# The last four token tiles of a down projection: two plain tiles, then a pair in seven products

## The chip, the core and the metric

The kernel runs on one core of a Trainium2 chip, in one launch. Time is device time in microseconds (us) of one execution; the kernel before took 725.91 us, the median of three runs (725.77 to 726.37). The engines are TensorE (PE, matrix products; its weight loads are listed as PEld), VectorE (DVE), ScalarE (ACT), GpSimd (POOL) and SyncE (SP), which issues the DMAs. Matrix products are accumulated in the banks of PSUM; all else that the engines work on lies in SBUF.

## The reference

One layer of an FNet block and a gated feed-forward block, on x of 2048 tokens by 448:

```
a = x_n @ dft_hid_re.T ; b = x_n @ dft_hid_im.T        # x_n = layernorm(x)
h = x + dft_seq_re @ a - dft_seq_im @ b
g = layernorm(h) @ w_gate ; u = layernorm(h) @ w_up    # 448 -> 1792
out = h + (gelu(g) * u) @ w_down                       # 1792 -> 448
```

All values are f32. The part that this document is about is the last product, called "down", for the last 512 tokens.

## The kernel before

**Precision.** f32 operands are split into two f16 parts, a high part (the value rounded) and a low part (what is left), so that one product takes three f16 matmuls: high x high, high x low, low x high. `hi_part` (L102) makes the high part on ScalarE, `lo_part` (L105) the low part on VectorE.

**Stages.** First the sequence and hidden DFT, up to about 330 us; then, in a loop of 56 steps over t (L979), gate and up: four groups q of 512 tokens by 14 chunks f of the 1792 hidden values. The down projection runs inside the same loop, one step of it for each step t from 14 on.

**Down in seven products.** Tokens are taken in pairs of tiles of 128 and the 448 output columns in two halves (HD = 224); the 1792 hidden values, 14 chunks of 128, are taken as 7 pairs of chunks (NC = 7). So one pair of token tiles is a 2 x 2 block product with 2 x 2 blocks, and `STRASSEN` (L147) lists seven products that replace the eight. Their left operands are the quarters A11 and A22 themselves and five sums of quarters, their right operands likewise the weights' (`wd`, made once and kept in SBUF, seven forms of each chunk). For a step d, `dn_sums` makes the five sums of a chunk pair (L804: two instructions on GpSimd, one on VectorE), `dn_split` their high and low parts, `dn_mm` the 21 matmuls of 224 columns. Six pairs p = 0 to 5 (the first 1536 tokens) are done so, seven steps each. The seven results lie in four PSUM banks, and `Drain` (L607) adds them into the four quarters of the output rows `hr`: `copy` moves two banks to SBUF on ScalarE, `sums` adds the four products in them by eight instructions on GpSimd, `bank2` and `bank3` add the other three on VectorE from PSUM. The method `banks01`, which adds four of the terms of the first two banks on VectorE instead, is there and is not called. The drain of pair p is hung into later steps of the loop through the table `side` (L947 to L959); that of the sixth pair, p = 5, falls on the last step, t = 55, and on what stands behind the loop.

**The last four tiles.** The last group, q = 3, has no later steps of the loop to run down in. Its hidden values are split into f16 as they come (`last_hi`, `last_lo`, into `h_last`), and behind the loop four tiles of 128 tokens are multiplied plainly by `last_mm` (L867): 14 chunks x 3 terms x 2 column halves, 84 matmuls of 224 columns for a tile. A tile is called by (j, g): the tokens g * 256 + j * 128 and on; j picks the rows `hr[6 + j]`. The weights that the seven-product form does not hold in plain form (quarters 12 and 21) are kept in `w_last`. The tiles go one after the other, (0,0), (0,1), (1,0), (1,1), each into a PSUM bank of its own; the last one is done half by half, in two banks, so that the first half can be added and stored under the second. `last_out` (L886) adds a bank into `hr` on VectorE and issues the store on SyncE.

**Order.** The program is scheduled by hand: each engine runs its instructions in the order in which they stand in the code, and waits only for what an instruction needs. Tiles of SBUF come from pools with a fixed number of buffers for a tag; a new tile waits until the last users of the old one are done. The tags that matter here: `hh` (two buffers, the hidden values of a group, and `h_last`), `hq` (two buffers, the hidden values of one step of the last group), `dn_s` (two buffers, five sums).

The code behind the loop:

```
    prev.c_last()
    for k in (1, 2, 0, 3):
        do(N_GU, k)
    ...
    for i in range(4):
        j, g = divmod(i, 2)
        last_mm(j, g, banks[i : i + 1] if i < 3 else banks[3:5])
```

Of the kernel before, what the change touches and what calls it, by code (L numbers as in the profile page):

```python
# [8 lines left out]
F16 = mybir.dt.float16  # L9
F32 = mybir.dt.float32  # L10
AF = mybir.ActivationFunctionType
ALU = mybir.AluOpType

P = 128
S, D, DF = 2048, 448, 1792
NT = S // P
NF = DF // P
# [10 lines left out]
W_SC = 256.0  # L28
H_SC = 0.25
# [3 lines left out]
def kernel(  # L33
# [6 lines left out]
    w_down: bass.AP,  # L40
    out: bass.AP,
):

# [23 lines left out]
    nc = tc.nc  # L69
    V, A, G, PE = nc.vector, nc.scalar, nc.gpsimd, nc.tensor  # L70
# [7 lines left out]
    ps_tr = ctx.enter_context(tc.tile_pool(name="ps_tr", bufs=1, space=bass.MemoryType.PSUM))  # L78
# [23 lines left out]
    def hi_part(dst, src, scale=1.0):  # L102
        A.activation(dst, src, AF.Copy, scale=scale)  # L103

    def lo_part(dst, src, hi, scale=1.0):  # L105
        if isinstance(scale, float) and scale == 1.0:
            V.tensor_sub(dst, src, hi)  # L107
        else:
            V.scalar_tensor_tensor(dst, src, scale, hi, op0=ALU.mult, op1=ALU.subtract)  # L109
# [37 lines left out]
    STRASSEN = [(0, 5), (1, 4), (3, 0), (2, 1), (6, 6), (5, 3), (4, 2)]  # L147
    HD = D // 2
# [349 lines left out]
    def at(where, n, *what):  # L498
        where.setdefault(n, []).extend(what)
# [5 lines left out]
    for k, f in enumerate(reversed(range(NF))):  # L505
        n = 17 + 3 * k
# [4 lines left out]
    for b in range(NB):  # L511
        for j in range(2):
            n = (b + 1) * NT + 1 + 6 * j
# [41 lines left out]
    for n in range(N_STEPS):  # L555
        b, c = divmod(n, NT)
# [42 lines left out]
    fpool = ctx.enter_context(tc.tile_pool(name="fpool", bufs=1, side="right", reuse_waits="tile"))  # L599
    wd = {n: fpool.tile([P, 2, 7, HD], F16, name=f"wd{n}") for n in range(NF // 2)}  # L600
# [99 lines left out]
    TQ = 2 * P  # L700
# [25 lines left out]
    def ftile(tag, bufs, name, n=TQ):  # L726
        return (fpool if tag == "u1" else late).tile([P, n], F32, tag=tag, bufs=bufs, name=name)

    hh, hq = {}, {}
# [67 lines left out]
    NC = NF // 2  # L797
    dn_s, dn_w, acc_d, hr = {}, {}, {}, {}
# [5 lines left out]
    def dn_sums(d):  # L804
        t = dn_hid(d)
        s = dn_s[d] = late.tile([P, 5, P], F32, tag="dn_s", bufs=2, name=f"dn_s{d}")
        G.tensor_add(s[:, 0:2], t[:, 0:2], t[:, 2:4])
        G.tensor_sub(s[:, 2:4], t[:, 1:4:2], t[:, 0:4:2])  # L808
        V.tensor_add(s[:, 4], t[:, 0], t[:, 3])
# [7 lines left out]
    outr = out.rearrange("(k g j p) d -> k j p g d", k=2, g=2, j=4)  # L817
# [19 lines left out]
    def dn_drain(p):  # L837
        v = [ftile(f"v{k}", 1, f"v{k}_{p}", D) for k in range(2)]
        return Drain(hr[p], acc_d.pop(p), v, 1.0 / (H_SC * W_SC))

    def dn_store(p):
        nc.sync.dma_start(outr[p // 4, p % 4], hr[p])
# [3 lines left out]
    last = {}  # L846
# [20 lines left out]
    def last_mm(j, g, banks):  # L867

        tok = slice(g * TQ + j * P, g * TQ + (j + 1) * P)
        one = len(banks) == 1  # L870
        for cs in ((0, 1),) if one else ((0,), (1,)):
            for f in range(NF):
                k, n = divmod(f, NC)
                for m, (lh, lw) in enumerate(((0, 0), (0, 1), (1, 0))):
                    for c in cs:
                        w = wd[n][:, lw, k] if c == k else last["w"][:, lw, n, k]
                        PE.matmul(  # L877
                            banks[0][:, c * HD : (c + 1) * HD] if one else banks[c][:, 0:HD],
                            last["h"][:, lh, f, tok],
                            w,  # L880
                            start=f == 0 and m == 0 and c == cs[0],
                            stop=f == NF - 1 and m == 2,
                            skip_group_check=True,
                        )

    def last_out(j, g, ps, c, n):  # L886
        p = 6 + j
        h = hr[p][:, g, c * HD : (c + n) * HD]
        V.scalar_tensor_tensor(h, ps[:, 0 : n * HD], 1.0 / (H_SC * W_SC), h, op0=ALU.mult, op1=ALU.add)
        nc.sync.dma_start(outr[p // 4, p % 4][:, g, c * HD : (c + n) * HD], h)  # L890

    def dn_ahead(t):

        if t in (NF - 4, NF - 1):
            dn_sums(int(t == NF - 1))
        if NF <= t < 6 * NC + 12:
            dn_sums(t - 12)

    N_GU = 4 * NF
# [4 lines left out]
    def do(t, k):  # L904
        for what in side.pop((t, k), ()):
            what()
# [25 lines left out]
    for t in range(3 * NF, N_GU):  # L932
        f = t % NF
        if f < NF - 1:
            n, k = divmod(f, 2)
# [11 lines left out]
    for p in range(6):  # L947
        t0 = NF + NC * p + NC - 1

        def begin(p=p):  # L950
            drains[p] = dn_drain(p)
            drains[p].copy()
            drains[p].bank2()

        at(side, (t0, 2), begin)
        at(side, (t0 + 1, 0), lambda p=p: drains[p].bank3())
        for n in range(4):
            at(side, (t0 + 1 + n, 3), lambda p=p, n=n: drains[p].sums((2 * n, 2 * n + 1)))
        at(side, (t0 + 4, 3), lambda p=p: dn_store(p))  # L959
# [12 lines left out]
    late = ctx.enter_context(tc.tile_pool(name="late", bufs=1, reuse_waits="tile"))  # L972
    ps_gu = ctx.enter_context(tc.tile_pool(name="ps_gu", bufs=1, space=bass.MemoryType.PSUM, reuse_waits="tile"))
    ps_dn = ctx.enter_context(tc.tile_pool(name="ps_dn", bufs=1, space=bass.MemoryType.PSUM, reuse_waits="tile"))
# [4 lines left out]
    for t in range(N_GU):  # L979
        q, f = divmod(t, NF)  # L980
# [26 lines left out]
        if q == 0:  # L1007
            dn_ahead(t)
            cur.xy()
            if f == NF - 2:  # L1010
                dn_split(0)
            prev = cur
            cur = GateUp(t + 1)
            cur.open()
            prev.yz()
            if d == -1:
                prev.c12_plus()
            continue
# [3 lines left out]
        dn_mm(d, range(0, 8))  # L1022
        cur.xy()
        dn_ahead(t)
        dn_mm(d, range(8, 18))
        do(t, 1)
# [9 lines left out]
            cur = GateUp(t + 1)  # L1036
            cur.open()
    prev.c_last()
    for k in (1, 2, 0, 3):
        do(N_GU, k)  # L1040
    banks = [(ps_tr, "tr"), (ps_gu, "X"), (ps_gu, "Y"), (ps_gu, "Z"), (ps_dn, "a0")]
    banks = [pool.tile([P, 512], F32, tag=tag, name=f"last_{tag}") for pool, tag in banks]
    for i in range(4):
        j, g = divmod(i, 2)
        last_mm(j, g, banks[i : i + 1] if i < 3 else banks[3:5])
        if i < 3:
            last_out(j, g, banks[i], 0, 2)
        else:
            last_out(j, g, banks[3], 0, 1)
            last_out(j, g, banks[4], 1, 1)  # L1050
        for t in range(N_GU + 1, N_GU + 4) if i == 0 else ():
            do(t, 3)
    assert not side


# [57 lines left out]
```

## Time and profile before

| | us |
|---|---|
| median of three runs | 725.91 (725.77 to 726.37) |
| the profiled execution: its own time | 726.24 |
| its span, first to last instruction | 724.4 |
| TensorE busy in the span | 719.4 |
| VectorE, ScalarE, GpSimd busy | 499.7, 271.8, 233.7 |

The profile is of one execution. "Span" is the time from its first to its last instruction; its own time is 1.84 us longer. Lines of the profile name a line of the kernel (L877), which can be that of a helper (L107 is the VectorE instruction in `lo_part`, wherever it was called from), then engine and operation, the tile written and the tiles read, partitions x elements and types. In the timeline the first two numbers are the start and the duration in us, "x84" merges 84 instructions, and the bracket tells how long the engine had been idle and which instruction ended that. In the list of groups come the summed busy time and the mean of one in ns. In the table of stretches come, after the bounds and the length, the busy time and count of PE, PEld, DVE, ACT and POOL, then the clock granted to TensorE (1.00 is full), the share of the DMA engines' time, and GB/s. Matmuls overlap in the pipeline: each is recorded with 0.26 us here, and the pace is read from the starts.

### The profile page before, as it was taken

The page shows a single profiled execution, that of the slowest core. Times are in us where ns is not written, and L with a number is a line of the kernel's source. Part 1 is how long each engine was busy: PE and PEld are TensorE (multiplying, and loading weights), DVE is VectorE, ACT ScalarE, POOL GpSimd, SP SyncE. Part 2 cuts the span into 40 slices and gives each one's busy share as a digit, 9 for nine tenths or more (in the row PEclk, how much of TensorE's full clock was granted, in tenths as well). Part 3 has the DMA queues.
Part 4 walks back from the last instruction along what each step waited for, and adds up shares of the span by engine and source line. Part 5 has one row for each costly group of instructions (what it writes and reads, how often), then busy time and mean ns, then how long its engine had stood idle before and what let it go on. Part 6 is the DMA issues. An engine that isn't in the chain of part 4 may idle for free.

```text
span 724.4 us, 13422 instructions
## 1 busy us (share of the span) xinstructions
PE 719.4 (99%) x5330; PEld 500.6 (69%) x5330; DVE 499.7 (69%) x1026; ACT 271.8 (38%) x535; POOL 233.7 (32%) x274
## 2 busy tenths in 40 slices
PE   9999999999999999999999999999999999999998
PEld 5444444444444444444488889999999999999998
DVE  6888657486674856440567768787787877989730
ACT  4444704156132452130344444443444434444410
POOL 0000000000000001000148855577686766758430
PEclk9999999999999999999999999999999999999999
DMA  8676565578657876711643564747538596555411
GB/s 277 223 231 219 183 223 189 196 215 277 233 196 218 293 242 248 274 67 61 254 153 128 177 210 167 187 174 223 180 124 253 172 205 217 198 198 205 153 39 39
DMA packets 63518, 139.83 MB, mean 193 GB/s; under 512 B 30304, under 2 KB 39520, under 8 KB 63456
## 3 DMA queue, kind: packets, MB, share of 16 engines
q1 hardware_dynamic: 63456, 138.99, 57.8%
q8 instruction: 41, 0.67, 0.4%
q14 instruction: 21, 0.17, 0.1%
HBM read 112.23 MB, written 20.19 MB: 183 GB/s over the span
## 4 chain that ended last, share of the span: by engine, by line
PE 98%; DMA 1%; DVE 1%; ACT 0%; issue 0%; SPq 0%; DVEq 0%
PE acc L414 35%; PE pY L714 14%; PE acc_d L662 11%; PE pZ L714 9%; PE pX L714 9%; PE y L479 9%; PE acc L428 6%; PE last_Y L877 1%; PE last_X L877 1%; PE last_tr L877 1%; DMA wr<-in_w_seq_dram 1%; PE last_a L877 1%; PE last_Z L877 1%; DVE c L724 0%; DVE dn_w L107 0%
## 5 line engine op out<-in xcount | busy, mean ns | idle before, releaser
L414 PE MATMUL acc<-ws,xs 128*128 128x512 f16 x1152 | 253.8, 379 | 0.2
L414 PEld LDWEIGHTS <-xs 128*128 128x128 f16 x1152 | 111.2, 98 | 138.6 <-issue 6.5
L714 PEld LDWEIGHTS <-gw 128*128 128x128 f16 x1911 | 186.7, 98 | 19.5 <-issue 0.7
L201 POOL TENSOR_TENSOR wd_s<-wd 128x448 f32<-128x448 f32 x7 | 7.9, 1132 | 352.0 <-DVE gu_w L109 274.2
L714 PE MATMUL pY<-hops,gw 128*128 128x256 f16 x833 | 114.0, 273 | 0.4 <-DVE u L724 0.2
L662 PE MATMUL acc_d<-wd,dn_w 128*128 128x224 f16 x882 | 105.1, 259 | 0.0
L109 DVE SCALAR_TENSOR_TENSOR ws<-wr,ws 128x1024 f16<-128x1024 f32 (+1 forms) x66 | 78.0, 1188 | 15.4 <-ACT ws L103 15.4
L103 ACT ACTIVATE ws<-wr 128x1024 f16<-128x1024 f32 (+1 forms) x66 | 66.2, 1021 | 57.8 <-DMA wr<-in_w_seq_dram 28.4
L662 PEld LDWEIGHTS <-dn_w 128*128 128x128 f16 x882 | 85.0, 98 | 2.9
L714 PE MATMUL pX<-hops,gw 128*128 128x256 f16 x539 | 74.9, 273 | 0.0
L714 PE MATMUL pZ<-hops,gw 128*128 128x256 f16 x539 | 73.7, 273 | 0.0
L724 DVE SCALAR_TENSOR_TENSOR u<-pY,u 128x256 f32<-128x256 f32 x112 | 46.9, 419 | 28.5 <-ACT c L788 18.6
L479 PE MATMUL y<-wh,z 128*128 128x448 f16 x336 | 65.7, 352 | 0.0
L487 DVE SCALAR_TENSOR_TENSOR hx<-y,hx 128x448 f32<-128x448 f32 x16 | 10.0, 625 | 76.1 <-PE y L479 76.1
L752 ACT ACTIVATE u<-pX 128x256 f32<-128x256 f32 x56 | 21.5, 383 | 89.0 <-PE pX L714 88.9
L479 PEld LDWEIGHTS <-z 128*128 128x128 f16 x336 | 32.8, 98 | 31.6 <-issue 0.4
L107 DVE TENSOR_TENSOR dn_w<-dn_s,dn_w 128x640 f16<-128x640 f32 x42 | 53.0, 1262 | 1.4 <-ACT dn_w L103 1.0
L781 POOL TENSOR_TENSOR hh<-hh,g 128x256 f32<-128x256 f32 x42 | 31.0, 739 | 64.2 <-DVE hh L724 50.6
L765 ACT ACTIVATE g<-pX 128x256 f32<-128x256 f32 x56 | 21.5, 384 | 74.9 <-PE pX L714 69.6
L790 POOL TENSOR_TENSOR hh<-hh,c 128x256 f32<-128x256 f32 x42 | 40.5, 964 | 17.1 <-ACT c L788 17.1
L428 PE MATMUL acc<-ws,xs 128*64 128x512 f16 x384 | 44.7, 381 | 0.0
L808 POOL TENSOR_TENSOR dn_s<-hh 128x256 f32<-128x256 f32 x42 | 43.4, 1034 | 0.0
(111 smaller groups left out, 844.1 us busy)
## 6 DMA issues: line engine op xcount, KB each, us to landing
gw<-w_dram SPq DMA_DIRECT2D x49, 896.0 KB, 4.8
wr<-in_w_seq_dram SPq DMA_DIRECT2D x62, 512.0 KB, 5.9
w_dram<-gu_w SPq DMA_DIRECT2D x14, 896.0 KB, 4.7
gu_raw<-in_w_gu_dram SPq DMA_DIRECT2D x28, 384.0 KB, 5.5
wd<-in_w_down_dram SPq DMA_DIRECT2D x14, 448.0 KB, 4.9
x<-in_x_dram SPq DMA_DIRECT2D x16, 224.0 KB, 3.3
hx<-in_x_dram SPq DMA_DIRECT2D x8, 448.0 KB, 7.0
h_dram<-hx SPq DMA_DIRECT2D x8, 448.0 KB, 3.1
```

Source lines behind the costliest of these rows:

```text
L103: A.activation(dst, src, AF.Copy, scale=scale)
L107: V.tensor_sub(dst, src, hi)
L109: V.scalar_tensor_tensor(dst, src, scale, hi, op0=ALU.mult, op1=ALU.subtract)
L414: PE.matmul(acc[b, 3 * part + k], xs[c][:, lx, k * P : (k + 1) * P], seq_w(n, lw, part), start=c == 0 and m == 0, stop=c == NT - 1 and m == 2,
L428: PE.matmul(acc[b, 6][64 * part : 64 * part + 64, :], xs[c][:, lx, 3 * P :], seq_w(n, lw, part), start=c == 0 and m == 0, stop=c == NT - 1 ...
L479: PE.matmul(y[:, :D], z[b][:, lz, k, i * P : (i + 1) * P], wh[:, lw, k, :], start=k == 0 and m == 0, stop=k == 6 and m == 2,)
L662: PE.matmul(acc[k // 2][:, k % 2 * HD : (k % 2 + 1) * HD], a_of(la, a), b_of(lb, b), start=first and m == 0 and k % 2 == 0, stop=last and ...
L714: PE.matmul(ps, w[:, wl, wa + ws, :], ops[:, m + ms, :], start=first and n == 0, stop=last and n == len(terms) - 1, skip_group_check=True,)
L724: V.scalar_tensor_tensor(dst, ps, SC, other, op0=ALU.mult, op1=ALU.add)
L790: G.tensor_mul(c22, c22, self.c12)
L808: G.tensor_sub(s[:, 2:4], t[:, 1:4:2], t[:, 0:4:2])
L877: PE.matmul(banks[0][:, c * HD : (c + 1) * HD] if one else banks[c][:, 0:HD], last["h"][:, lh, f, tok], w, start=f == 0 and m == 0 and c = ...
```

## The change

Behind the loop, tiles (1,0) and (1,1) are done first, plainly and whole, in two banks. Then tiles (0,0) and (0,1) are done as a pair in seven products. Their operands are made from `h_last`: `last_sums` adds high and low part of each quarter (two VectorE instructions for a chunk pair, into a `hq` buffer) and makes the five sums from that (one instruction on GpSimd, two on VectorE); `last_split` makes the high part on ScalarE and the low part on VectorE, into `last_a`, which takes a `hh` buffer. Chunk pairs 0 and 1 are made before the first plain tile's matmuls in the code, 2 to 6 behind the first tile's output. For the two products whose left operand is a quarter itself, the matmuls read `h_last`. Chunk pairs 0 to 3 go through all seven products in turn; then each product takes its chunk pairs 4 to 6, and as products get done VectorE adds them into the output quarters (twelve adds for seven products) and each quarter is stored after its last add.

The drain of the sixth down pair is no longer hung into the last step: it stands behind the loop as a whole, with four of its terms by `banks01` on VectorE, and four instead of eight instructions on GpSimd.

```diff
+    def last_sums(n):
+        if n == 0:
+            a = fpool.tile([P, NF, 2 * TQ], F32, tag="hh", bufs=2, name="last_a")
...
+        v = late.tile([P, 4, P], F32, tag="hq", bufs=2, name=f"last_v{n}")
+        for k in range(2):
+            f = n + k * NC
+            V.tensor_add(v[:, 2 * k : 2 * k + 2], h[:, 0, f], h[:, 1, f])
+        s = late.tile([P, 5, P], F32, tag="dn_s", bufs=2, name=f"last_s{n}")
+        G.tensor_add(s[:, 0:2], v[:, 0:2], v[:, 2:4])
+        V.tensor_sub(s[:, 2:4], v[:, 1:4:2], v[:, 0:4:2])
+        V.tensor_add(s[:, 4], v[:, 0], v[:, 3])
+    def last_split(n):
+        s, a = last.pop(("s", n)), last["a"][:, n]
+        hi_part(a[:, 0], s)
+        lo_part(a[:, 1], s, a[:, 0])
+    def last_pair_mm(k, n, banks):
+        a, b = STRASSEN[k]
+        bank, c = banks[k]
+        for m, (la, lb) in enumerate(((0, 0), (0, 1), (1, 0))):
+            PE.matmul(
+                bank[:, c * HD : (c + 1) * HD],
+                last["a"][:, n, la, a - 2] if a > 1 else last["h"][:, la, n + a * NC, a * TQ : a * TQ + P],
+                wd[n][:, lb, b, :],
...
+        if p == 5:
+            continue
...
-    for k in (1, 2, 0, 3):
+    for k in (1, 2):
         do(N_GU, k)
...
-    for i in range(4):
-        j, g = divmod(i, 2)
-        last_mm(j, g, banks[i : i + 1] if i < 3 else banks[3:5])
...
+    drain = dn_drain(5)
+    drain.copy()
+    drain.banks01()
+    drain.bank2()
+    drain.bank3()
+    drain.sums(range(4))
+    dn_store(5)
+    names = [(ps_tr, "tr"), (ps_gu, "X"), (ps_gu, "Y")] + [(ps_dn, f"a{k}") for k in range(4)]
...
+    for n in range(2):
+        last_sums(n)
+        last_split(n)
+    for g in range(2):
+        last_mm(1, g, banks[g : g + 1])
+    last_out(1, 0, banks[0], 0, 2)
+    for n in range(2, NC):
+        last_sums(n)
+        last_split(n)
+        if n == 4:
+            last_out(1, 1, banks[1], 0, 2)
+    banks = [(banks[3], 0), (banks[3], 1), (banks[4], 0), (banks[4], 1), (banks[5], 0), (banks[6], 0), (banks[2], 0)]
+    for n in range(4):
+        for k in range(7):
+            last_pair_mm(k, n, banks)
...
+    users = {1: ((0, 1, 1), (0, 3, 1), (1, 0, -1), (1, 2, -1)), 3: ((2, 2, 1), (3, 1, 1), (2, 3, -1), (3, 0, -1))}
+    users.update({4: ((4, 0, 1), (4, 3, 1)), 5: ((5, 0, -1),), 6: ((6, 3, 1),)})
+    for k in range(7):
+        for n in range(4, NC):
+            last_pair_mm(k, n, banks)
+        for m, dst, sign in users.get(k, ()):
+            bank, c = banks[m]
+            h, ps = drain.x[dst], bank[:, c * HD : (c + 1) * HD]
+            V.scalar_tensor_tensor(h, ps, sign * drain.sc, h, op0=ALU.mult, op1=ALU.add)
+            if (m, dst) in ((2, 2), (3, 1), (5, 0), (6, 3)):
+                g, c = divmod(dst, 2)
+                nc.sync.dma_start(outr[1, 2][:, g, c * HD : (c + 1) * HD], h)
```

More of the change, by code (lines that the diff above doesn't have):

```diff
@@ L890, in last_out @@
         nc.sync.dma_start(outr[p // 4, p % 4][:, g, c * HD : (c + n) * HD], h)
+    def last_sums(n):
+        if n == 0:
+            a = fpool.tile([P, NF, 2 * TQ], F32, tag="hh", bufs=2, name="last_a")
+            a = a.rearrange("p f t -> p (f t)")[:, : NC * 5 * P].bitcast(F16)
+            last["a"] = a.rearrange("p (n l a t) -> p n l a t", n=NC, l=2, a=5)
+        h = last["h"].rearrange("p l f (g j t) -> p l f g j t", g=2, j=2)[:, :, :, :, 0]
+        v = late.tile([P, 4, P], F32, tag="hq", bufs=2, name=f"last_v{n}")
[6 more added lines that the diff above has]
+        V.tensor_add(s[:, 4], v[:, 0], v[:, 3])
+        last["s", n] = s
+    def last_split(n):
[10 more added lines that the diff above has]
+                wd[n][:, lb, b, :],
+                start=n == 0 and m == 0 and c == 0,
+                stop=n == NC - 1 and m == 2,
+                skip_group_check=True,
+            )
     def dn_ahead(t):
@@ L1038 @@
     prev.c_last()
-    for k in (1, 2, 0, 3):
+    for k in (1, 2):
         do(N_GU, k)
-    banks = [(ps_tr, "tr"), (ps_gu, "X"), (ps_gu, "Y"), (ps_gu, "Z"), (ps_dn, "a0")]
-    banks = [pool.tile([P, 512], F32, tag=tag, name=f"last_{tag}") for pool, tag in banks]
-    for i in range(4):
-        j, g = divmod(i, 2)
-        last_mm(j, g, banks[i : i + 1] if i < 3 else banks[3:5])
[L1046 to L1052, printed above, removed]
+    drain = dn_drain(5)
[6 more added lines that the diff above has]
+    names = [(ps_tr, "tr"), (ps_gu, "X"), (ps_gu, "Y")] + [(ps_dn, f"a{k}") for k in range(4)]
+    banks = [pool.tile([P, 512], F32, tag=tag, name=f"last_{tag}") for pool, tag in names]
+    for n in range(2):
[13 more added lines that the diff above has]
+            last_pair_mm(k, n, banks)
+    drain = Drain(hr[6], (), (), 1.0 / (H_SC * W_SC))
+    users = {1: ((0, 1, 1), (0, 3, 1), (1, 0, -1), (1, 2, -1)), 3: ((2, 2, 1), (3, 1, 1), (2, 3, -1), (3, 0, -1))}
[10 more added lines that the diff above has]
+                nc.sync.dma_start(outr[1, 2][:, g, c * HD : (c + 1) * HD], h)
     assert not side
```

## The prediction

> **What bounds the kernel now.** I read the page first, then the chain of waits over the last 40 us, then the timeline and the stretches there. The page says that TensorE is the bound, and the chain that it is so to the end:
>
> ```profile
> span 724.4 us, 13422 instructions
> PE 719.4 (99%) x5330; PEld 500.6 (69%) x5330; DVE 499.7 (69%) x1026; ACT 271.8 (38%) x535; POOL 233.7 (32%) x274
> ...
> 689.14 8.05 PE last_tr L877 x84
> 697.19 8.05 PE last_X L877 x84
> 705.24 8.05 PE last_Y L877 x84
> 713.29 4.03 PE last_Z L877 x42
> 717.31 4.04 PE last_a L877 x42
> 721.35 0.02 issue
> 721.37 0.39 DVE hr L889
> ```
>
> From 689.14 to 721.35 TensorE runs the four last tiles without a gap: 84 matmuls in 8.05 us are 95.8 ns each. Behind them come one VectorE add of 0.39 us, ended at 721.76, and 2.64 us of storing up to the span's end. The other engines do next to nothing meanwhile:
>
> ```profile
> 700.00:710.00 10.00, 10.00 (x107) 10.00 (x105) 0.62 (x1) 0.00 (x0) 0.00 (x0) 1.00 0.12 46
> ```
>
> So matmuls removed here shorten the kernel one for one, unless what feeds the new ones comes late.
>
> **What goes.** Two plain tiles (168 matmuls) become 7 products x 7 chunks x 3 terms = 147, and the instruction order of the changed program has these numbers: that it leaves out 21 matmuls is certain. At 95.8 ns they are 2.01 us.
>
> **What comes: operands that must be made at the very end.** Five of the seven products take sums of four quarters of the hidden values, which did not exist before. For each of seven chunks VectorE adds hi+lo twice (128x256, from f16), GpSimd adds 256 columns, VectorE subtracts 256 and adds 128, ScalarE rounds 640 to f16, VectorE subtracts 640 for the low part. They stand in program order, one chunk wholly behind the other: VectorE's low part of chunk n waits for ScalarE, which waits for GpSimd and VectorE, and all of chunk n+1 is queued behind it. Nothing overlaps between chunks; this is a chain. Prices, as shortest/median/longest:
>
> ```profile
> L309 DVE TENSOR_TENSOR gu_s<-gu_raw x14: 417/419/421, 86.5 to 306.9; 128x256 f32<-128x256 f32 x14
> ...
> L809 DVE TENSOR_TENSOR dn_s<-hh x42: 281/282/814, 411.6 to 674.8; 128x128 f32<-128x128 f32 x42
> L807 POOL TENSOR_TENSOR dn_s<-hh x42: 722/911/1309, 412.2 to 673.3; 128x256 f32<-128x256 f32 x42
> ...
> L103 ACT ACTIVATE dn_w<-dn_s x42: 722/726/737, 420.2 to 678.2; 128x640 f16<-128x640 f32 x42
> L107 DVE TENSOR_TENSOR dn_w<-dn_s,dn_w x42: 812/1343/1347, 421.3 to 679.0; 128x640 f16<-128x640 f32 x42
> ```
>
> The long values are GpSimd and VectorE standing in each other's way:
>
> ```profile
> 653.27 0.71 DVE L107 TENSOR_TENSOR dn_w<-hh,dn_w 128x256 f16<-128x256 f32 x1
> 653.91 1.34 DVE L107 TENSOR_TENSOR dn_w<-dn_s,dn_w 128x640 f16<-128x640 f32 x1
> ...
> 653.66 0.91 POOL L790 TENSOR_TENSOR hq<-hq,c 128x256 f32<-128x256 f32 x1
> 654.53 1.31 POOL L807 TENSOR_TENSOR dn_s<-hh 128x256 f32<-128x256 f32 x1
> ```
>
> Each is late by about what the other still had to do (0.81 to 1.34, 0.72 to 1.31): whoever comes second waits until some 0.13 us before the first one's recorded end, and then takes its own time. The same rows show a VectorE instruction starting 0.07 before the recorded end of an independent one. Handoffs:
>
> ```profile
> 688.39 0.42 DVE L724 SCALAR_TENSOR_TENSOR hq<-pY,u 128x256 f32<-128x256 f32 x1
> 688.95 0.73 POOL L781 TENSOR_TENSOR hq<-hq,g 128x256 f32<-128x256 f32 x1 [3.90 <-DVE hq L724]
> 688.96 0.42 DVE L724 SCALAR_TENSOR_TENSOR c<-pZ,u 128x256 f32<-128x256 f32 x1
> 689.48 0.42 ACT L788 ACTIVATE c<-c 128x256 f32<-128x256 f32 x1 [0.34 <-DVE c L724]
> ...
> 690.85 0.63 ACT L103 ACTIVATE h_last<-hq 128x512 f16<-128x512 f32 x1 [0.95 <-POOL hq L790]
> 691.51 1.09 DVE L107 TENSOR_TENSOR h_last<-hq,h_last 128x512 f16<-128x512 f32 x1 [0.26 <-ACT h_last L103]
> ```
>
> VectorE to GpSimd takes 0.14 us (688.81 to 688.95), VectorE to ScalarE 0.10, ScalarE to VectorE 0.03. One chunk, from its first add at 0: second add 0.35 to 0.77; subtraction 0.80 to 1.22; GpSimd asks at 0.91, gets its turn at 1.09, ends at 1.81; the 128-column add waits for it to 1.68 and ends at 1.96; ScalarE 2.06 to 2.79; low part 2.82 to 3.63; the next chunk starts at 3.56. I take 3.55 us per chunk. Bounds: without any standing in the way 3.17 (0.77 + 0.14 + 0.72 + 0.04 + 0.73 + 0.03 + 0.81 - 0.07); with GpSimd first and both VectorE instructions behind it 3.75. No row has a VectorE add of two f16 inputs into f32; by the 256-column row it is 0.42, and were it twice as fast the two would save about 0.36 per chunk, 2.8 at the lowest.
>
> **When the chain starts.** The drain of the sixth down pair moves behind the loop, and its four terms on GpSimd go to VectorE as well:
>
> ```profile
> 688.16 0.97 ACT L621 ACTIVATE v<-acc_d 128x448 f32<-128x448 f32 x2
> 690.15 1.10 DVE L625 SCALAR_TENSOR_TENSOR hr<-acc_d,hr 128x224 f32<-128x224 f32 x3
> 690.77 5.43 POOL L653 TENSOR_TENSOR hr<-hr,v 128x224 f32<-128x224 f32 x8
> L107 DVE TENSOR_TENSOR h_last<-hq,h_last x14: 692/886/1090, 614.1 to 691.5; 128x512 f16<-128x512 f32 x14
> ```
>
> The low part at 691.51 still waits for the last rounding; GpSimd's sums now come after it, so it takes 0.69 and not 1.09, to 692.20. Then eight adds: an independent one follows after 0.31, a dependent one after 0.41 (0.41 + 0.31 + 0.38 = 1.10 for three), together from 692.13 to 694.87. All of it, the two copies and GpSimd's four sums (half of 5.43) lie under the plain tiles, whose matmuls need none of them; what it costs is that the first chunk starts only at 694.80. The two plain tiles' outputs stand in VectorE's queue behind chunks 1 and 4, 0.55 each (0.62 less the overlap):
>
> ```profile
> L889 DVE SCALAR_TENSOR_TENSOR hr<-last_X,hr x1: 625/625/625, 705.3 to 705.3; 128x448 f32<-128x448 f32 x1
> ```
>
> Their matmuls are long done by then, at 697.19 and 705.24. Chunk 6 is ready at 694.80 + 7 x 3.55 + 2 x 0.55 + 0.07 = 720.82; chunks 3, 4 and 5 by the same count at 709.62, 713.17 and 717.27.
>
> **What TensorE meets.** The pair starts at 705.24; four chunks of 21 matmuls end at 713.29, all in time. Then each product takes chunks 4 to 6. The first two products use the stored halves and need no sums: 18 matmuls to 715.01. The third does three for chunk 4 (715.30) and then stands: two matmuls of chunk 5 at 716.43, one at 717.27, two of chunk 6 at 719.98, the last at 720.82 to 720.95. Four products, 36 matmuls, 3.45 us, remain: 724.40. VectorE, freed at 720.75, has twelve output adds (0.38, 0.31 if independent): four to 722.06, four to 723.40, two to 724.12, one to 724.53, the last to 724.94. That is 3.18 behind 721.76; the 2.64 behind it stays, as the last piece stored is as large as before, and no store is in its way:
>
> ```profile
> 697.88 0.34 SPq L890 DMA_DIRECT2D out_dram<-hr  x1
> ```
>
> On SyncE's queue the sixth pair's store now stands ahead of the tiles' and is due by 695, GpSimd's and VectorE's end on that pair; the last two pieces follow 0.41 apart, and one takes 0.34 to issue. Sum: -2.01 of matmuls, +5.06 of TensorE waiting (724.40 against 719.34), +0.13 of adds queued at the end (0.54 behind the last matmul, 0.41 before). On the profiled execution's 726.24 this gives 729.42, on the median of 725.91, 0.33 below it, 729.1.
>
> **The clock while TensorE stands.** From 715.30 to 720.95 it has six matmuls, 0.57 us in 5.65. The trace has one stretch of that kind, its end:
>
> ```profile
> 722.50:723.50 1.00, 0.00 (x0) 0.00 (x0) 0.00 (x0) 0.00 (x0) 0.00 (x0) 1.00 0.36 115
> 723.50:724.00 0.50, 0.00 (x0) 0.00 (x0) 0.00 (x0) 0.00 (x0) 0.00 (x0) 0.91 0.00 0
> 724.00:724.40 0.40, 0.00 (x0) 0.00 (x0) 0.00 (x0) 0.00 (x0) 0.00 (x0) 0.50 0.00 0
> ...
> 1.37 6.02 PE L97 MATMUL pw<-ident 128*128 128x128 f16 x56 [1.37 <-POOL sign_t L88]
> ```
>
> A share of 0.91 over 0.5 us that ends at 0.50 puts the fall at 723.91, 2.56 us after the last matmul. The longest gap forecast is 717.37 to 719.98, 2.61 us, in a stretch that is 90% idle; I take it that the clock falls to half. The start of the kernel bounds the way back: 56 transposes of 128 columns took 107 ns each, slower than 224 columns at 95.8, so work was slow for up to 6 us there. At half speed the last 37 matmuls cost up to 3.54 us more, less 0.14 by which VectorE would end later anyway: between 0 and 3.4, and I take the middle, 1.7, as the rows say nothing of how soon it recovers. Forecast: 729.1 + 1.7 = 730.8.
>
> [...]
>
> **The rivals.** (1) *The gain comes*: faster. The chain of sums must keep ahead of TensorE: chunk 6 ready by 715.6, so at most (715.6 - 694.80 - 1.17)/7 = 2.80 us per chunk. Then the end moves by the 2.01 of matmuls: 723.9. For it speaks only the unknown f16 add; against it that the bare instructions of a chunk make 3.02 even with no handoff. (2) *The chain is late but the clock holds*: 729.1. For it, that six matmuls break the gap; against it, the 723.91 fall. (3) *The chain is late by little*: at 3.17 per chunk, chunk 6 is ready at 718.2 and the end comes 0.5 later than now, 726.4, no change. Against it, the rows above, where GpSimd and VectorE hardly ever miss each other. (4) *Both ends bad*: 3.75 per chunk (1.4 more) and a clock at half to the end: 733.9.
>
> **How the numbers follow.** Forecast, chain late and clock fallen: 0.52, time 730.8, its own range 729.6 to 732.6. Rival 2: 0.28, 728.2 to 729.8. Rival 3: 0.10, rival 1: 0.04, rival 4: 0.06. The range 728.0 to 732.6 leaves out rivals 1, 3 and 4, 0.20 together. What a measurement of this kernel can tell is about 0.2%, 1.45 us: faster is under 724.5 (0.04, rival 1), the same up to 727.4 (0.08 of rival 3), slower 0.88 (the rest).
>
> **What would show it.** Right: VectorE's low parts of `last_a` some 3.55 us apart, each waiting for ScalarE; TensorE waiting for them from about 715 on; a granted clock under 1.00 in the last 8 us. Wrong: low parts 2.8 apart and no idle TensorE; or a product waiting for something else than the sums, as the banks, which this working takes to be free 10 us early; or a full clock with matmuls 95.8 ns apart to the end, which leaves 729.1.

## The result, and the profile after

| | before | after |
|---|---|---|
| median of six runs each, us | 726.00 (725.77 to 726.95) | 731.21 (730.54 to 732.24) |
| after over before | | 1.0072, 95% interval 1.0061 to 1.0083 |
| the profiled execution: own time, span | 726.24, 724.4 | 731.05, 729.2 |
| TensorE behind the loop, start of the first matmul to end of the last, us | 32.4 | 37.2 |

The changed kernel is slower by 0.7%, some 5 us. Of the page after, these are the busy times, and the shares of the chain of waits by engine:

```profile
span 729.2 us, 13457 instructions
PE 719.7 (99%) x5309; PEld 499.0 (68%) x5309; DVE 521.4 (72%) x1074; ACT 276.4 (38%) x542; POOL 237.3 (33%) x277
...
PE 91%; DVE 5%; DMA 2%; ACT 1%; issue 1%; POOL 0%; SPq 0%; ACTq 0%; DVEq 0%; POOLq 0%
```

The same shares before:

```profile
PE 98%; DMA 1%; DVE 1%; ACT 0%; issue 0%; SPq 0%; DVEq 0%
```

21 matmuls are gone (5330 to 5309), yet TensorE is as long busy as before (719.7 and 719.4): that number hides matmuls that ran slower, recorded with up to 395 ns where the shortest of the pair has 258. Of the seven points that TensorE lost in the chain, VectorE took four and ScalarE one. Line numbers are two higher than before, for two blank lines. The timeline of the changed kernel shows the last low part of `h_last`, then one chunk of the new chain, on the three engines that make it, and then the end of the last chunk and the output adds (start, length, engine, line, instruction, and in brackets how long the engine had stood and for what):

```profile
691.56 0.69 DVE L109 TENSOR_TENSOR h_last<-hq,h_last 128x512 f16<-128x512 f32 x1 [1.28 <-ACT h_last L105]
...
694.88 0.75 DVE L904 TENSOR_TENSOR last_v<-h_last 128x256 f32<-128x256 f16 x2
695.66 0.43 DVE L907 TENSOR_TENSOR last_s<-last_v 128x256 f32<-128x256 f32 x1
696.01 0.81 DVE L908 TENSOR_TENSOR last_s<-last_v 128x128 f32<-128x128 f32 x1
697.68 0.82 DVE L109 TENSOR_TENSOR last_a<-last_s,last_a 128x640 f16<-128x640 f32 x1 [0.86 <-ACT last_a L105]
698.43 0.75 DVE L904 TENSOR_TENSOR last_v<-h_last 128x256 f32<-128x256 f16 x2
...
720.04 0.83 DVE L109 TENSOR_TENSOR last_a<-last_s,last_a 128x640 f16<-128x640 f32 x1 [0.86 <-ACT last_a L105]
720.79 1.28 DVE L1116 SCALAR_TENSOR_TENSOR hr<-last_a,hr 128x224 f32<-128x224 f32 x4
...
726.25 0.39 DVE L1116 SCALAR_TENSOR_TENSOR hr<-last_Y,hr 128x224 f32<-128x224 f32 x1 [0.47 <-PE last_Y L921]
```

```profile
695.71 0.96 POOL L906 TENSOR_TENSOR last_s<-last_v 128x256 f32<-128x256 f32 x1 [0.97 <-DVE last_v L904]
...
696.91 0.74 ACT L105 ACTIVATE last_a<-last_s 128x640 f16<-128x640 f32 x1 [4.52 <-DVE last_s L908]
```

Between two chunks nothing overlaps: one starts at 694.88, the next at 698.43, 3.55 us later. VectorE's 128-column add is recorded with 0.81 us; in e4 below, where GpSimd has no part in it, the same add takes 0.28. So the record holds a wait behind GpSimd, and ScalarE waits for the add. Seven low parts from 697.68 to 720.04, with two output adds of 0.53 between, are (22.36 - 1.06)/6 = 3.55 us apart. TensorE at the same place:

```profile
714.90 0.45 PE L921 MATMUL last_a<-wd,last_a 128*128 128x224 f16 x3
716.52 0.36 PE L921 MATMUL last_a<-wd,last_a 128*128 128x224 f16 x2 [1.17 <-ACT last_a L105]
717.38 0.27 PE L921 MATMUL last_a<-wd,last_a 128*128 128x224 f16 x1 [0.49 <-DVE last_a L109]
720.07 0.37 PE L921 MATMUL last_a<-wd,last_a 128*128 128x224 f16 x2 [2.42 <-ACT last_a L105]
720.93 4.42 PE L921 MATMUL last_a<-wd,last_a 128*128 128x224 f16 x28 [0.49 <-DVE last_a L109]
725.19 1.03 PE L921 MATMUL last_Y<-wd,last_a 128*128 128x224 f16 x9
```

It stands four times for chunks 5 and 6, and the 37 matmuls behind take 5.3 us, where the pace of before makes it 3.7 (36 x 95.8 ns and 0.26 for the last). The stretches say why (busy us and count of PE, PEld, DVE, ACT, POOL, then the granted clock, DMA share, GB/s):

```profile
718.00:720.00 2.00, 0.00 (x0) 0.00 (x0) 1.15 (x2) 0.72 (x1) 0.90 (x1) 1.00 0.00 0
720.00:722.00 2.00, 1.44 (x8) 1.00 (x9) 1.96 (x5) 0.01 (x1) 0.00 (x0) 0.69 0.00 0
722.00:724.00 2.00, 2.00 (x13) 1.62 (x11) 1.05 (x5) 0.00 (x0) 0.00 (x0) 0.50 0.00 0
724.00:726.00 2.00, 2.00 (x22) 1.92 (x20) 1.38 (x4) 0.00 (x0) 0.00 (x0) 0.95 0.35 115
```

0.69 in a stretch of 2 us that ends at 0.50 is a fall at 720.76; 0.95 in the last is a return at 724.2. The clock fell just as the work came, and stayed down for 3.4 us.

### The profile page after: what moved, and what is told of

The parts are those of the page before. It is cut to its first block, busy times and chain, and to the rows that moved or that the text cites. A ratio compares the mean times of both kernels' runs of the same rounds, so it can differ in the third digit from the quotient of the medians.

```text
span 729.2 us, 13457 instructions
## 1 busy us (share of the span) xinstructions
PE 719.7 (99%) x5309; PEld 499.0 (68%) x5309; DVE 521.4 (72%) x1074; ACT 276.4 (38%) x542; POOL 237.3 (33%) x277
## 4 chain that ended last, share of the span: by engine, by line
PE 91%; DVE 5%; DMA 2%; ACT 1%; issue 1%; POOL 0%; SPq 0%; ACTq 0%; DVEq 0%; POOLq 0%
PE acc L416 33%; PE pY L716 14%; PE acc_d L664 11%; PE pX L716 9%; PE pZ L716 9%; PE y L481 9%; PE acc L430 6%; DMA x<-in_x_dram 1%; ACT last_a L105 1%; DVE last_s L908 1%; DVE last_a L109 1%; DVE last_v L904 1%; PE last_a L921 1%; DMA wr<-in_w_seq_dram 1%; DVE last_s L907 0%
```

## The experiments

Ratios are to the kernel before on the same chip, with their 95% intervals. A difference between two rows, or between a row and the changed kernel, is known to some 1.0 to 1.2 us either way.

| kernel | median, us | before there | ratio |
|---|---|---|---|
| e1, sums overlapped | 724.10 | 726.16 | 0.9969 (0.9956 to 0.9981) |
| e2, gaps filled with matmuls | 729.76 | 726.16 | 1.0044 (1.0031 to 1.0056) |
| e3, the two moves alone | 726.37 | 726.16 | 1.0001 (0.9992 to 1.0010) |
| e4, sums without GpSimd | 728.75 | 726.16 | 1.0035 (1.0022 to 1.0048) |
| e5, e1 with chunks in turn | 726.69 | 726.59 | 1.0003 (0.9994 to 1.0012) |
| e6, changed kernel with chunks in turn | 729.33 | 726.59 | 1.0042 (1.0029 to 1.0054) |
| e7, drain between the sums | 727.35 | 726.59 | 1.0015 (1.0006 to 1.0024) |

**e1: break the chain.** The same instructions in another order: the sums of the next chunk go ahead of the low part of this one.

```diff
+    last_sums(0)
     for n in range(2):
-        last_sums(n)
+        last_sums(n + 1)
         last_split(n)
...
     for n in range(2, NC):
-        last_sums(n)
+        if n + 1 < NC:
+            last_sums(n + 1)
         last_split(n)
```

> Theory (the sums are one unbroken chain, and TensorE waits for it): with the sums of chunk n+1 queued ahead of the low part of chunk n, the low parts come about 2.6 us apart instead of 3.55, chunk 6 is ready near 714.3 instead of 720.87, TensorE never stands, the clock stays at 1.00, and the time is 726.0 - 2.0 + 0.1 = 724.1 us (723.7 to 724.6). Rival (the pair form is slow in itself: its banks, its output adds, or VectorE and GpSimd in each other's way): low parts stay 3.3 us apart or more, or TensorE waits for something else, and the time stays above 727.

724.10 us, as forecast. From the timeline of e1, VectorE and then TensorE:

```profile
698.03 0.81 DVE L109 TENSOR_TENSOR last_a<-last_s,last_a 128x640 f16<-128x640 f32 x1
698.76 0.74 DVE L904 TENSOR_TENSOR last_v<-h_last 128x256 f32<-128x256 f16 x2
699.54 0.43 DVE L907 TENSOR_TENSOR last_s<-last_v 128x256 f32<-128x256 f32 x1
699.88 0.82 DVE L908 TENSOR_TENSOR last_s<-last_v 128x128 f32<-128x128 f32 x1
700.62 0.81 DVE L109 TENSOR_TENSOR last_a<-last_s,last_a 128x640 f16<-128x640 f32 x1
...
712.08 1.76 DVE L109 TENSOR_TENSOR last_a<-last_s,last_a 128x640 f16<-128x640 f32 x2
...
714.33 3.61 PE L921 MATMUL last_a<-wd,last_a 128*128 128x224 f16 x36
717.78 1.03 PE L921 MATMUL last_Y<-wd,last_a 128*128 128x224 f16 x9
```

The low parts are 2.59 apart (698.03 to 700.62), and VectorE waits for nobody: the brackets are gone. The last chunk is ready at 713.84, before the third product, the first that needs sums here, begins with chunk 4 at 714.33, and the matmuls run through. So with the order of VectorE's queue changed the whole loss goes, and the 21 matmuls bring what they are worth. This version is faster than both kernels. (The 128-column add still stands 0.53 behind GpSimd; it no longer matters.)

**e2: keep the waits, keep the clock.** Nothing is made faster; matmuls whose bank nobody reads fill two of the gaps.

```diff
+    fill = ps_gu.tile([P, 512], F32, tag="Z", name="last_fill")
...
+            for i in range((0, 10, 24)[n - 4] if k == 2 else 0):
+                PE.matmul(
+                    fill[:, 0:HD], last["h"][:, 0, 0, 0:P], wd[0][:, 0, 0, :], start=True, stop=True, skip_group_check=True
+                )
             last_pair_mm(k, n, banks)
```

> 34 matmuls into a bank that nobody reads fill TensorE's two gaps before chunks 5 and 6 of the third product; no wait is removed. Theory (the clock falls because TensorE stands): granted clock 1.00 to the end, the last 37 matmuls 95.8 ns apart, the time 731.2 - 1.8 = 729.4 us (729.0 to 729.8), and its runs lie within 1 us of each other as those of the kernel before do, not 1.7. Rival (the clock is no cost, VectorE's adds set the end anyway): 731 and the same spread.

729.76 us; TensorE's timeline and two stretches of e2:

```profile
717.07 2.46 PE L1114 MATMUL last_fill<-wd,h_last 128*128 128x224 f16 x24
719.66 0.37 PE L921 MATMUL last_a<-wd,last_a 128*128 128x224 f16 x2
720.52 2.86 PE L921 MATMUL last_a<-wd,last_a 128*128 128x224 f16 x28 [0.49 <-DVE last_a L109]
```

```profile
715.00:720.00 5.00, 4.17 (x39) 3.19 (x36) 3.24 (x7) 1.47 (x2) 0.98 (x2) 1.00 0.00 0
720.00:722.00 2.00, 1.51 (x17) 1.49 (x17) 1.90 (x6) 0.00 (x0) 0.00 (x0) 1.00 0.00 0
```

28 matmuls from 720.52 take 2.86 us; in the changed kernel 28 took 4.42. 34 matmuls more made the kernel shorter: the difference of the two ratios, 0.0028, is 2.0 us. The two profiled runs give less: the 37 matmuls took 3.7 us here (720.52 to 724.23) and 5.3 in the changed kernel, 1.6 apart. That is the clock's share; the other 3.2 us stay with the wait. The part on the spread was missed and tells nothing: e2's five runs lie within 1.14 us, but the kernel before spread over 1.5 on that chip.

**e3: the moves without the pair.** Tiles (1,0) and (1,1) first, the drain behind the loop, then two more plain tiles. Against the loop of the kernel before:

```diff
-        j, g = divmod(i, 2)
+        j, g = 1 - i // 2, i % 2
         last_mm(j, g, banks[i : i + 1] if i < 3 else banks[3:5])
```

> Four plain tiles as before, tiles (1,0) and (1,1) first, and the sixth pair's drain behind the loop as in the changed kernel; no pair form at the end. Theory: both moves lie under the plain tiles, time as before, 726.0 (725.6 to 726.4). Rival (the moved drain or the order of the tiles costs part of the 5.2 us): 727 or more.

726.37 us, ratio 1.0001; the chain of e3 has the four tiles without a gap, as before:

```profile
689.63 8.05 PE last_tr L879 x84
...
717.81 4.04 PE last_a L879 x42
721.85 0.02 issue
721.87 0.39 DVE hr L891
```

From 689.63 to 721.85 are 32.22 us, before 32.21. The moves alone cost nothing that can be measured; what the drain costs it costs only as a thing ahead of the sums, which e7 tells.

**e4: no handoff to GpSimd.**

```diff
-        G.tensor_add(s[:, 0:2], v[:, 0:2], v[:, 2:4])
+        V.tensor_add(s[:, 0:2], v[:, 0:2], v[:, 2:4])
```

> The changed kernel with GpSimd's addition of 256 columns done by VectorE: no handoff to GpSimd and nobody in the way. Theory: a chunk takes 0.77 + 0.03 + 0.35 + 0.35 + 0.28 + 0.10 + 0.74 + 0.03 + 0.82 - 0.07 = 3.40 us instead of 3.55, chunk 6 is ready 1.0 us earlier (719.8), TensorE still waits; the time falls by about that, to 730.1, or to 729 where the clock then holds in part of the runs. Rival (the two engines in each other's way are the main cost): low parts 3.0 apart or less, the time under 727.5.

728.75 us: faster than forecast, on the theory's side of it but not by its number. The timeline of e4 has the low parts 3.30 apart, not 3.40 (VectorE, then ScalarE):

```profile
696.04 0.28 DVE L908 TENSOR_TENSOR last_s<-last_v 128x128 f32<-128x128 f32 x1
697.13 0.83 DVE L109 TENSOR_TENSOR last_a<-last_s,last_a 128x640 f16<-128x640 f32 x1 [0.80 <-ACT last_a L105]
...
700.43 0.82 DVE L109 TENSOR_TENSOR last_a<-last_s,last_a 128x640 f16<-128x640 f32 x1 [0.80 <-ACT last_a L105]
...
696.36 0.74 ACT L105 ACTIVATE last_a<-last_s 128x640 f16<-128x640 f32 x1 [4.27 <-DVE last_s L908]
```

Between the low parts VectorE's five instructions and ScalarE's one still follow each other. Most of the 0.10 us is the handoff to ScalarE: 0.04 (696.32 to 696.36), where the working had 0.10. Seven times 0.25 us is 1.8; the ratios make it 2.7 (0.0037 of 726), give or take 1.2, so the two agree. The two profiled runs are 2.3 us apart: 1.8 of the chain, 0.3 because the first sums, whose start the edit does not touch, came at 694.58 and not at 694.88, and 0.2 because the clock fell at another moment, 718.2, so that the last 28 matmuls took 4.20 us and not 4.42. So GpSimd's share of the chain is a fourteenth of a chunk's 3.55 us; the rest is that nothing overlaps.

**e5 and e6: the product-by-product end, with the sums in time and late.** Both let all seven chunks go through the seven products in turn; e5 is made from e1, e6 from the changed kernel.

```diff
-    for n in range(4):
+    for n in range(NC):
         for k in range(7):
             last_pair_mm(k, n, banks)
...
     for k in range(7):
-        for n in range(4, NC):
-            last_pair_mm(k, n, banks)
         for m, dst, sign in users.get(k, ()):
```

> The overlapped sums of e1, but all seven chunks go through the seven products in turn, with no product by product at the end. TensorE ends as in e1; the twelve output adds can start only as the last 21 matmuls end. Theory (the product-by-product end is worth the adds that it hides): the last add ends 2.8 us behind the last matmul instead of 0.45, time 724.1 + 2.3 = 726.4 us, so that the pair form alone brings nothing over the kernel before. Rival (VectorE's adds keep up anyway): 724.1.

726.69 us, ratio 1.0003. The timeline of e5:

```profile
717.86 3.77 DVE L1116 SCALAR_TENSOR_TENSOR hr<-last_a,hr 128x224 f32<-128x224 f32 x11 [3.54 <-PE last_a L921]
721.54 0.38 DVE L1116 SCALAR_TENSOR_TENSOR hr<-last_Y,hr 128x224 f32<-128x224 f32 x1
...
718.81 0.45 PE L921 MATMUL last_Y<-wd,last_a 128*128 128x224 f16 x3
```

VectorE stands 3.54 us, then has all twelve adds one behind the other, to 721.92, 2.7 us past TensorE's recorded end at 719.26. Without the product-by-product end the pair form has no gain that can be measured.

> The changed kernel with its late chain of sums, all seven chunks in turn. Theory: here the product-by-product end holds the matmuls of chunks 4 and 5 back behind chunk 6; in turn, they fill TensorE's waiting, only 13 matmuls are left once chunk 6 is ready at 720.9, TensorE ends at 722.2, and the output adds on VectorE, which follow chunk 6 directly, set the end at 724.9 whether the clock falls or not: 731.2 - 1.7 = 729.5 us (729.1 to 729.9). Rival (the end is worth 2.3 us here as it is with the sums in time): 733 or more.

729.33 us, ratio 1.0042: here the same edit is a gain of 0.0030, 2.2 us, over the changed kernel. The timeline of e6:

```profile
717.47 0.37 PE L921 MATMUL last_a<-wd,last_a 128*128 128x224 f16 x2 [0.60 <-ACT last_a L105]
...
721.01 0.37 PE L921 MATMUL last_a<-wd,last_a 128*128 128x224 f16 x2 [0.69 <-ACT last_a L105]
721.88 1.13 PE L921 MATMUL last_a<-wd,last_a 128*128 128x224 f16 x10 [0.49 <-DVE last_a L109]
722.84 0.45 PE L921 MATMUL last_Y<-wd,last_a 128*128 128x224 f16 x3
...
721.73 3.76 DVE L1114 SCALAR_TENSOR_TENSOR hr<-last_a,hr 128x224 f32<-128x224 f32 x11
725.41 0.38 DVE L1114 SCALAR_TENSOR_TENSOR hr<-last_Y,hr 128x224 f32<-128x224 f32 x1
```

No gap is longer than 0.69 us, 13 matmuls are left behind chunk 6, and the adds, not TensorE, set the end. The granted clock is 1.00 in every stretch from 714.00 to 724.00, 0.7 us past TensorE's recorded end at 723.29, so the changed kernel's fall is part of what is gained. The order that is right for sums in time is the wrong one for sums that come late: it queues the matmuls of chunks 4 and 5 behind chunk 6.

**e7: the drain between the sums.** Of the eight adds, three go between the sums and the low part of chunk 0, three of chunk 1, two of chunk 2; GpSimd's four sums go two with chunk 0 and two with chunk 1.

```diff
     drain.copy()
+    adds = ((0, 1, -1.0), (3, 0, 1.0), (0, 3, -1.0), (3, 2, -1.0), (0, 4, 1.0), (0, 5, -1.0), (3, 4, 1.0), (3, 6, 1.0))
-    drain.banks01()
-    drain.bank2()
-    drain.bank3()
-    drain.sums(range(4))
-    dn_store(5)
...
     for n in range(2):
         last_sums(n)
+        for what in adds[3 * n : 3 * n + 3]:
+            drain.add(*what)
+        drain.sums((2 * n, 2 * n + 1))
         last_split(n)
...
     for n in range(2, NC):
         last_sums(n)
+        if n == 2:
+            for what in adds[6:]:
+                drain.add(*what)
+            dn_store(5)
         last_split(n)
```

> The changed kernel, with VectorE's eight adds and GpSimd's four sums of the sixth pair's drain put between the sums and the low part of chunks 0 to 2, where VectorE waits 0.86 us for ScalarE anyway. Theory (the drain's 2.7 us ahead of the chain count in full): the chain starts at 692.2 instead of 694.9, loses some 0.4 back, chunk 6 is ready at 718.6, 2.3 us earlier; time 731.2 - 2.3 = 728.9 us with the clock falling as it does now, 727.2 where it holds. Rival (the drain is hidden): 731.

727.35 us, between the two numbers of the theory, because its runs are of two kinds. The time of each of ten runs, with the mean clock granted over the run:

```
clock 1.000:           726.79 726.83 726.96 726.98 727.31 727.39 727.60
clock 0.997 or 0.998:  728.46 728.49 728.84
```

The middle ones are 726.98 and 728.49, 1.5 us apart; 727.2 and 728.9 were forecast with the clock held and fallen. That the fall lies under the work in the slower runs is read from their times: the mean alone does not say where it lies, as the profiled run of e6 has 0.998 with its fall behind the last matmul. The profiled run of e7 is one of the first kind, and its last 28 matmuls take 2.86 us as in e2, at a granted clock of 1.00 from 714.00 to 724.00 (VectorE, then TensorE):

```profile
691.32 0.69 DVE L109 TENSOR_TENSOR h_last<-hq,h_last 128x512 f16<-128x512 f32 x1 [1.28 <-ACT h_last L105]
691.92 0.75 DVE L904 TENSOR_TENSOR last_v<-h_last 128x256 f32<-128x256 f16 x2
...
717.40 0.37 PE L921 MATMUL last_a<-wd,last_a 128*128 128x224 f16 x2 [2.00 <-ACT last_a L105]
718.26 2.86 PE L921 MATMUL last_a<-wd,last_a 128*128 128x224 f16 x28 [0.49 <-DVE last_a L109]
```

The sums now follow directly behind the last low part of `h_last`, 0.60 us after its start; in the changed kernel the way from there to the sums is 3.32 (691.56 to 694.88). TensorE's last 28 matmuls start 26.94 us behind that low part, there 29.37: 2.4 us sooner. The drain's 2.7 us ahead of the sums counted in full, and 0.3 of them came back as adds between.

## Why the prediction was right, point by point

- **The gain** of 2.01 us from 21 matmuls is real: e1 gets it, 0.0031 of 726 or 2.2 us (1.4 to 3.2). In the changed kernel it is more than eaten.
- **The chain's start and pitch** were right almost to the digit: 694.80 forecast, 694.88 measured; 3.55 us per chunk in both; chunk 6 ready at 720.82 and 720.87. The unknown add of two f16 inputs took 0.42 as the f32 row did (second add ended 0.75 behind the first's start, 0.77 forecast). That one chunk waits behind the other was the reason: e1 removes it, and all of the loss goes. That the start agrees to 0.1 us is partly luck: it was taken over from one run, whose last low part of `h_last` starts at 691.51, and in the profiled runs with the new code it starts anywhere from 690.98 (e1) to 692.50 (e6). The pitch is the same in all that have this order (3.55 between the last two low parts of e2, e6 and e7).
- **Who stands in whose way**: the 128-column add waiting for GpSimd was forecast to end 1.96 behind the chunk's start, and ended 1.94 behind it. Handing over to GpSimd took 0.08 in the first two chunks and 0.14 or 0.15 in the other five, and GpSimd ended 1.79 or 1.80 behind the chunk's start in all seven (1.81 forecast): its add is recorded with 0.90 to 0.96, where the shortest of before has 0.72, so that it waited too, by the working for the subtraction. e4 shows this part small, 0.25 of 3.55 us.
- **The drain ahead of the chain**: 2.7 us forecast (692.13 to 694.80), 2.72 by e7 (3.32 against 0.60).
- **TensorE's waits**: the longest gap was forecast with 2.61 us and recorded with 2.42, at the same place.
- **The clock**: that it falls was right, in the profiled run at 720.76; its price, 1.7 taken from the middle between 0 and 3.4, is 1.5 by e7 and 1.6 (traces) to 2.0 (times) by e2. The middle was a choice that no row supported, so that it came out this near is luck. How soon the clock comes back was open too: the start of the kernel, which the working took as a bound, has a granted clock of 1.00 in the trace (0.00 to 7.40), and the changed kernel's came back 3.4 us after the fall. The price is a term of its own: rival 2 (the clock holds) was forecast 3.2 us above the kernel before, and e2, which holds it, is 3.2 above (0.0044 of 726).
- **The sum** was 730.8 for a measured 731.21. The last add ends at 726.64, which is 724.94 + 1.7; to the digit, that is luck, for the two reasons above. What is not in the sum is that some runs seem to lose two stretches of the clock, as the last section tells; it would move the median up by a part of 1.4 us.
- **Not foreseen**: that the product-by-product end, worth 2.5 us when the sums are in time (e5 against e1, 0.0034), costs 2.2 when they are late (e6), the clock's fall included. The working had the order of the matmuls right, but did not ask what the other order would do.

## What to carry to other kernels

A helper that goes through three engines and back, called once for each piece in a queue that runs in order, is a chain: its price here was the sum of all its steps for each piece, 3.55 us, not the busy time of the engine with most of it (VectorE, 2.81 us recorded for a chunk). Calling the first half for the next piece ahead of the second half of this one took 0.96 us per chunk here and turned 0.7% lost into 0.3% gained, with the same instructions. And TensorE's waits cost more here than their length: behind them the granted clock was 0.50 for 3.4 us, and 37 matmuls took 5.3 us, where e2 has 3.7.

## What the runs showed of the hardware

The longest gap of TensorE before the clock fell was 2.42 us in the profiled run of the changed kernel, and 2.17 in that of e4. In e4 the clock is 0.82 from 715.00 to 720.00 and 0.59 from 720.00 to 722.00, which puts the fall at 718.2 and the return at 721.6; in both kernels it came back 3.4 us after the fall.

How little TensorE had to do does not tell these runs apart. In the 3.4 us up to the fall it was busy for 0.64 us in the changed kernel and for 0.9 in e4. In the profiled run of e7 it was busy for 0.9 us from 714.86 to 718.26, with a gap of 2.00 in it, and the clock is 1.00 there and up to 724.00. What decides it no run shows.

Runs of one program differ in what they lose: the six runs of the changed kernel have mean clocks of 0.998 (730.54, 730.71, 731.05 us) and 0.995 (731.37, 732.12, 732.24). By estimate, a stretch of 3.4 us at 0.50 takes 0.0023 off the mean of a run of 731 us, so the second kind fits two such stretches; its middle run is 1.4 us longer. The second stretch is read from the means alone, as the runs beside the profiled one have no trace here; and three runs of a kind are few, where six runs of the kernel before already spread over 1.2 us.
